# VectorE's every eighth product moved to the front of its step, with a one-element copy on GpSimd in its place there

## The chip, the cores and the metric

The kernel runs on one NeuronCore of one Trainium2 chip. The metric is device time in microseconds for one execution. Five engines matter here: TensorE (PE in the profile, with its weight loads as PEld), VectorE (DVE), ScalarE (ACT), GpSimd (POOL) and SyncE (SP), which only issues DMAs. GpSimd issues DMAs too.

## The reference

Agent attention over two batches of 12480 tokens with 49 agents, followed by a feed-forward layer whose activation is a ratio of two polynomials. Cut to what matters:

```python
a2k = softmax(scale * agents @ k.T);  agent_v = a2k @ v          # 49 x 128, per batch
x   = softmax(scale * q @ agents.T) @ agent_v                    # 24960 x 128
h   = x @ w_in                                                   # 24960 x 2048
P   = a[0] + a[1]*h + a[2]*h**2 + a[3]*h**3
Q   = 1 + abs(b[0])*abs(h) + abs(b[1])*h**2
out = (P / (Q + 1e-6)) @ w_out                                   # 24960 x 128
```

## The kernel before

**Tiles and stages.** A first stage of some 60 us computes the attention of the agents over batch 0. It also folds `agent_v` into `w_in`, so that `h` comes straight from the 49 attention weights of a token (tile `pT`) and the folded weights (`m_hi`, `m_lo`). From then on one loop does the feed-forward layer. The work is cut into 49 blocks of 512 tokens by 16 chunks of 128 hidden columns, 784 pieces, and three pieces make a **unit**: 128 partitions by 1536 elements. There are 262 units (`NU`), and step `i` of the loop starts unit `i`.

**One unit.** TensorE writes `h` into a PSUM slot (`mm1`, lines 494 and 495; there are two slots, so `mm1` of unit i+2 must wait until unit i's slot has been read). ScalarE squares it into the tile `u` (line 559). VectorE makes the denominator `w` (`dve2`, line 588) and then the first part of the numerator `u` (`dve1`, line 580); both read the slot, and `dve1` is its last reader. ScalarE turns `w` of a pair of units into its reciprocal by logarithm and exponential (lines 573 and 575). Six steps after the unit's start `u` is multiplied with `w`, and seven steps after it (`LAG`) TensorE multiplies the product with `w_out` (`mm2`, line 502).

**Who does that product.** Seven units in eight are multiplied by GpSimd (line 644, `u <- u * w`). A constant has to be added to `u` before that, and GpSimd issues an accumulating DMA for it (`add_om`, lines 600 and 605), for a pair of units at every second step; it waits for `dve1` of the younger unit of the pair. Every eighth unit (`u % 8 == 7`) and the last seven are multiplied by VectorE (`dve_last`, line 593), which adds the constant in the same instruction. Such a unit `u` is multiplied at step j = u + 6, called a **product step** here; there are 31 of them before the tail.

**Order.** The schedule is written out by hand: each engine runs its instructions in the order in which the loop names them. In a product step VectorE had: `dve2(j)`, `dve1(j)`, what `run_hold("DVE")` holds, then `dve_last(u)`. What `run_hold` runs are pieces of two side streams that `attend` spreads over the steps, one piece per step: the attention of the agents over batch 1 (scores until about 350 us, then a stage until about 600 us in which GpSimd subtracts maxima at line 253), and the attention of the tokens, in 25 groups of 1024 tokens. A group's piece on VectorE is `q_ev` (lines 422 and 423), later `q_sum` (432, 433); on GpSimd it is line 440, and a step later lines 441 and 442. A group comes every 10.67 units, so that three groups fill 32 units, and with them four product steps. The **four places** of a product step in this cycle are called D, B, A and C here, in order of time: at D, `q_ev` stands in the step's hold; at A, GpSimd has lines 441 and 442 in the step before; at C, line 440 stands in the step's hold on GpSimd.

GpSimd's queue at a product step: the product of unit u-1 (step j-1), its held pieces, nothing of its own in step j, then in step j+1 the product of unit u+1 and the `add_om` that waits for `dve1(j)`; in the queue that `add_om` stands ahead of the product.

Of the kernel before, what the change touches and what calls it, by code (L numbers as in the profile page):

```python
# [11 lines left out]
F32 = mybir.dt.float32  # L12
# [68 lines left out]
def agent_attention_rational_moe(  # L81
# [12 lines left out]
    PE, ACT, DVE, POOL, SP = nc.tensor, nc.scalar, nc.vector, nc.gpsimd, nc.sync  # L94

    const = ctx.enter_context(tc.tile_pool(name="const", bufs=1))
# [12 lines left out]
    cab = const.tile([128, 6], F32, name="cab")  # L109
    b_abs = const.tile([128, 2], F32, name="b_abs")  # L110
    cf = const.tile([128, 96], F32, name="cf")
    mcol = const.tile([128, 1], F32, name="mcol")
    flag = const.tile([128, 1], I32, name="flag")
    c0_t = const.tile([128, 1], F32, name="c0_t")
# [343 lines left out]
    NU = len(units)  # L458

    def on_pool(u):  # L460
        return u % ON_DVE != ON_DVE - 1 and u < NU - LAST_DVE

    def main(wk, streams, fast):
# [4 lines left out]
        def span(u):  # L468
            return width(units[u][0] // NFC)

        def view(k, u):
            n = len(units[u])
            if k == "w":
                return wt[u // 2 % (NWT if fast else 2)][:, u % 2, :n, :span(u)]
            if k == "x" and not fast:
                return wt[3][:, u % 2, :n, :span(u)]
            return ut[u // 2 % (NUT // 2)][:, u % 2, :n, :span(u)]
# [5 lines left out]
        def mm1(u):  # L483
            s = slots[u % 2]
            for j, n in enumerate(units[u]):
                blk, fc = divmod(n, NFC)
                f = slice(fc * 128, (fc + 1) * 128)
                t, n = blk * BT, width(blk)
                cut = min(max(N - t, 0), n)
                for b, lo, hi in ((0, 0, cut), (1, cut, n)):  # L490
                    if lo < hi:
                        assert (b, fc // 4) in made
                        rhs = pT_t[blk // 2][:, (blk % 2) * BT + lo:(blk % 2) * BT + hi]
                        PE.matmul(s[:, j, lo:hi], lhsT=m_hi[b][:KR, f], rhs=rhs, start=True, stop=False)  # L494
                        PE.matmul(s[:, j, lo:hi], lhsT=m_lo[b][:KR, f], rhs=rhs, start=False, stop=True)  # L495

        def mm2(u):
            done = None
            g = view("u", u)
            for j, n in enumerate(units[u]):  # L500
                blk, fc = divmod(n, NFC)
                PE.matmul(outs[blk % 2][:, :width(blk)], lhsT=wo[:, fc, :], rhs=g[:, j, :], start=fc == 0, stop=fc == NFC - 1)  # L502
                if fc == NFC - 1:
                    done = blk
            return done

        def out_ev(blk):
            n = width(blk)
            o = ring(at_p, 1, [128, BT], F32, "o")[:, :n]
            (DVE.tensor_copy if blk in OUT_DVE else ACT.copy)(out=o, in_=outs[blk % 2][:, :n])  # L510
            SP.dma_start(out=outT[:, blk * BT:blk * BT + n], in_=o)
# [9 lines left out]
        def run_hold(e):  # L521
            fs = hold[e]
            hold[e] = []
            for f in fs:
                f()
# [29 lines left out]
        def act(i):  # L555
            if i < NU:
                h, w, x, y = slot(i), view("w", i), view("x", i), view("u", i)
                if fast:
                    ACT.activation(out=x, in_=h, func=AF.Square, scale=arm["xb"], bias=1.0)  # L559
                else:  # L560
                    ACT.activation(out=x, in_=h, func=AF.Abs)
                    ACT.activation(out=y, in_=h, func=AF.Identity, scale=cab[:, 3:4], bias=cab[:, 2:3])
                    POOL.tensor_scalar(out=w, in0=x, scalar1=b_abs[:, 1:2], scalar2=b_abs[:, 0:1], op0=ALU.mult, op1=ALU.add)
            if fast:
                p = (i - 3) // 2
                ready = pair(p) if 0 <= p and 2 * p < NU else []
                ln, ex = i % 2 == 1, i % 2 == 0
            else:
                ready = [view("w", i - 1)] if 0 <= i - 1 < NU else []
                ln = ex = True  # L570
            for r in ready:
                if ln:
                    ACT.activation(out=r, in_=r, func=AF.Ln, bias=arm["lb"])  # L573
                if ex:
                    ACT.activation(out=r, in_=r, func=AF.Exp, scale=-1.0)  # L575

        def dve1(i):
            h, x, y = slot(i), view("x", i), view("u", i)
            if fast:
                DVE.scalar_tensor_tensor(out=y, in0=x, scalar=co["kap_l"], in1=h, op0=ALU.add, op1=ALU.mult)  # L580
            else:
                DVE.tensor_tensor(out=y, in0=h, in1=y, op=ALU.mult)
                DVE.scalar_tensor_tensor(out=y, in0=y, scalar=cab[:, 1:2], in1=h, op0=ALU.add, op1=ALU.mult)

        def dve2(i):
            h, x, w = slot(i), view("x", i), view("w", i)
            if fast:
                DVE.scalar_tensor_tensor(out=w, in0=h, scalar=co["mu_l"], in1=x, op0=ALU.max, op1=ALU.add)  # L588
            else:
                DVE.tensor_tensor(out=w, in0=w, in1=x, op=ALU.mult)  # L590

        def dve_last(u):
            DVE.scalar_tensor_tensor(out=view("u", u), in0=view("u", u), scalar=arm["om"], in1=view("w", u), op0=ALU.add, op1=ALU.mult)  # L593


        def add_om(u):
            us = [v for v in (u, u + 1) if 0 <= v < NU and on_pool(v)]
            if len(us) == 2 and all(len(units[v]) == UJ and span(v) == BT for v in us):
                t = ut[u // 2 % (NUT // 2)].rearrange("p h j t -> p h (j t)")
                POOL.dma_start(out=t, in_=omd.unsqueeze(1).to_broadcast([128, 2, UJ * BT]), accum_op=ALU.add)  # L600
                return
            for v in us:
                n, m = len(units[v]), span(v)
                src = omd.rearrange("p (j t) -> p j t", j=UJ)[:, :n, :m]
                POOL.dma_start(out=view("u", v), in_=src, accum_op=ALU.add)  # L605
# [19 lines left out]
        for i in range(NU + lag):  # L625
            act(i)
            run_hold("ACT")
            g = i - gap
            fin = [g] if 0 <= g < NU and not on_pool(g) else []
            if i == NU - 1:  # L630
                dve_last(fin.pop())
            if i < NU:
                dve2(i)
                dve1(i)
            run_hold("DVE")
            for u in fin:
                dve_last(u)
            if done is not None:
                out_ev(done)
                done = None  # L640
            if i % 2 == 0:
                add_om(i - 2)
            if 0 <= g < NU and on_pool(g):
                POOL.tensor_tensor(out=view("u", g), in0=view("u", g), in1=view("w", g), op=ALU.mult)  # L644
            run_hold("POOL")
            if i + 1 < NU:
                mm1(i + 1)
            cur = 0
            if i >= lag:
                done = mm2(i - lag)  # L650
                cur = units[i - lag][-1] // NFC
            soon = i >= lag and units[min(i + 1 - lag, NU - 1)][-1] // NFC != cur
            used = i > 0 and attend(outs[1 - cur % 2], units[min(i + 1, NU - 1)][-1] // NFC, done is not None, soon, i)
            if i < lag and not used:
                for _ in range(DUM):
                    PE.matmul(outs[0][:, :BT], lhsT=wo[:, 0, :], rhs=wi[:, :BT], start=True, stop=True)
# [85 lines left out]
    with tc.manual_schedule():  # L742
# [136 lines left out]
        def rest(fast):  # L879
            for n, d in (("q", q_t), ("pT", pT_t)):  # L880
                d.clear()
                d.update(state[n])
            for n, r in rings.items():
                r[1] = turns.get(n, 0)
            if fast:
                xb = ACT.alloc_register("xb")
                ACT.reg_load(xb, co["xb"][0:1, :].bitcast(I32))
                arm.update(om=co["om_l"], lb=co["lb_l"], xb=xb)
            else:
                arm.update(om=cab[:, 0:1], lb=c0_t)  # L890
            main(wk, [q_stream(1), w_stream(fast), a2k_stream(kv, 1, G1)], fast)
# [42 lines left out]
```

## Time and profile before

| | |
|---|---|
| median of 3 runs | 1305.13 us (1304.97 to 1305.24) |
| the profiled execution | 1304.85 us, its span 1303.1 us |
| PE busy | 1219.9 us, 94% |
| DVE busy | 1171.6 us, 90% |
| ACT busy | 1155.6 us, 89% |
| POOL busy | 1028.3 us, 79% |
| line 593, DVE, the product on VectorE | 38 instructions, 608 to 10062 ns, median 1812 ns |
| line 644, POOL, the product on GpSimd | 224 instructions, mean 3911 ns |

Four engines are busy for most of the time, and they wait for each other in a ring (slot, square, `dve2` and `dve1`, slot). So a busy share alone doesn't tell which one sets the pace; that has to be read from the stage. The median of VectorE's product is 1.81 us, its longest instance over five times that.

### The profile page before, as it was taken

The numbers are of one execution on the slowest core, as the hardware profiler recorded it, in microseconds if no ns is written. First come the engines' busy times: TensorE is split into PE (matmuls) and PEld (weight loads), VectorE is DVE, ScalarE is ACT, GpSimd is POOL, SyncE is SP. The second block draws the span as 40 slices with busy tenths as digits, with TensorE's granted clock in tenths as the row PEclk, the third lists the DMA queues.
The fourth block names the chain that finished last, engine by engine and source line by source line (L and its number), as shares of the span: only waits on it lengthen the run. The fifth ranks groups of instructions, "written<-read, shape, count | busy, mean of one in ns | idle before, by whom it ended". The sixth has DMA issues, their size and how long they took to land.

```text
span 1303.1 us, 14400 instructions
## 1 busy us (share of the span) xinstructions
PE 1219.9 (94%) x5396; PEld 711.1 (55%) x5396; DVE 1171.6 (90%) x865; ACT 1155.6 (89%) x752; POOL 1028.3 (79%) x511
## 2 busy tenths in 40 slices
PE   7979989999899989999899997999799997999998
PEld 6745545555455545555456554555455554555554
DVE  6898898998998898989999989999999989899996
ACT  3479979999799987999799997999799997999995
POOL 4538968878789887888678887888688887798893
PEclk8989989999899999999899998999899998999999
DMA  9569979998699996988879886889879886899990
GB/s 358 206 143 185 195 171 204 201 197 184 147 190 206 214 199 138 206 185 166 173 147 184 181 181 133 181 177 191 173 156 181 183 179 130 175 181 181 185 178 26
DMA packets 53263, 233.58 MB, mean 179 GB/s; under 512 B 4800, under 2 KB 5312, under 8 KB 53184
## 3 DMA queue, kind: packets, MB, share of 16 engines
q0 software_dynamic: 30720, 176.17, 70.9%
q1 hardware_dynamic: 22464, 56.39, 12.2%
q8 instruction: 45, 0.74, 0.2%
q14 instruction: 34, 0.28, 0.1%
HBM read 218.98 MB, written 13.57 MB: 178 GB/s over the span
## 4 chain that ended last, share of the span: by engine, by line
PE 71%; DVE 19%; ACT 5%; issue 2%; POOL 2%; DMA 1%; SPq 0%; DVEq 0%; ACTq 0%; POOLq 0%
PE outb L502 41%; PE slot L494 12%; PE slot L495 11%; DVE u L593 6%; DVE u L580 4%; DVE w L588 4%; ACT u L559 3%; PE outb L213 2%; POOL u L644 1%; PE outb L447 1%; ACT w L573 1%; PE outb L271 1%; DMA k<-kT 1%; PE bank L213 1%; PE outb L300 0%
## 5 line engine op out<-in xcount | busy, mean ns | idle before, releaser
L644 POOL TENSOR_TENSOR u<-u,w 128x1536 f32<-128x1536 f32 x224 | 840.4, 3911 | 0.0
L502 PE MATMUL outb<-u,wo 128*128 128x512 f32 (+1 forms) x1568 | 728.9, 601 | 49.8 <-DVE u L593 46.5
L588 DVE SCALAR_TENSOR_TENSOR w<-slot,cf,u 128x1536 f32<-128x1536 f32 (+1 forms) x262 | 472.1, 1802 | 90.2 <-ACT u L559 77.0
L502 PEld LDWEIGHTS outb<-u,wo 128*128 128x128 f32 x1568 | 299.6, 192 | 336.8 <-issue 250.2
L580 DVE SCALAR_TENSOR_TENSOR u<-u,cf,slot 128x1536 f32<-128x1536 f32 (+1 forms) x262 | 472.2, 1802 | 9.3
L559 ACT ACTIVATE u<-slot 128x1536 f32<-128x1536 f32 (+1 forms) x262 | 382.0, 1458 | 52.0 <-PE slot L495 32.8
L494 PE MATMUL slot<-pT,m_hi 113*128 113x512 f32 (+3 forms) x800 | 369.9, 464 | 14.9 <-DVE u L580 14.7
L573 ACT ACTIVATE w<-w,cf 128x3072 f32<-128x3072 f32 (+1 forms) x134 | 375.1, 2802 | 0.0
L575 ACT ACTIVATE w<-w 128x3072 f32<-128x3072 f32 (+1 forms) x134 | 362.9, 2710 | 0.0
L495 PE MATMUL slot<-pT,m_lo 113*128 113x512 f32 (+3 forms) x800 | 312.0, 391 | 0.0
L600 POOL DMA_DIRECT2D u<-omd x96 | 121.0, 1260 | 166.9 <-DVE u L580 97.6
L494 PEld LDWEIGHTS slot<-pT,m_hi 113*128 113x128 f32 x800 | 151.2, 189 | 93.5 <-DVE u L580 41.4
L495 PEld LDWEIGHTS slot<-pT,m_lo 113*128 113x128 f32 x800 | 151.5, 189 | 49.4 <-issue 25.9
L593 DVE SCALAR_TENSOR_TENSOR u<-u,cf,w 128x1536 f32<-128x1536 f32 (+2 forms) x38 | 119.2, 3147 | 0.0
L510 ACT COPY o<-outb 128x512 f32<-128x512 f32 (+1 forms) x40 | 23.6, 590 | 51.2 <-PE outb L502 51.2
L605 POOL DMA_DIRECT2D u<-omd x32 | 31.7, 990 | 40.2 <-DVE u L580 23.0
L447 PEld LDWEIGHTS outb<-ident,p 128*113 128x113 f32 x187 | 26.7, 178 | 25.2 <-issue 20.6
L213 PEld LDWEIGHTS outb<-ag,q 128*64 128x64 f32 x748 | 24.5, 141 | 17.8 <-issue 9.5
L447 PE MATMUL outb<-ident,p 128*113 128x128 f32 x187 | 28.3, 274 | 1.5 <-DVE o L510 1.5
L453 ACT CAST pT<-outb 113x512 fp32r<-113x512 f32 (+1 forms) x47 | 28.2, 600 | 0.1
L213 PE MATMUL outb<-ag,q 128*64 128x49 f32 x748 | 27.6, 228 | 0.0
L440 POOL TENSOR_TENSOR e<-e,qs 128x392 f32<-128x392 f32 (+1 forms) x25 | 26.4, 1057 | 1.5 <-DVE qs L433 0.7
(138 smaller groups left out, 476.1 us busy)
## 6 DMA issues: line engine op xcount, KB each, us to landing
u<-omd POOLq DMA_DIRECT2D x96, 1536.0 KB, 11.7
u<-omd POOLq DMA_DIRECT2D x32, 768.0 KB, 7.3
q<-qT SPq DMA_DIRECT2D x24, 512.0 KB, 7.3
outT<-o SPq DMA_DIRECT2D x48, 256.0 KB, 5.8
v<-vP SPq DMA_DIRECT2D x24, 258.0 KB, 7.1
k<-kT SPq DMA_DIRECT2D x24, 256.0 KB, 6.6
v<-vP SPq DMA_DIRECT2D x9, 645.0 KB, 11.4
k<-kT SPq DMA_DIRECT2D x8, 640.0 KB, 9.7
```

The lines of the kernel that those rows point to most:

```text
L213: PE.matmul(bank[lo:hi, o:o + A], lhsT=toks[:, lo:hi], rhs=ag[:, b * A:(b + 1) * A], start=True, stop=True)
L494: PE.matmul(s[:, j, lo:hi], lhsT=m_hi[b][:KR, f], rhs=rhs, start=True, stop=False)
L495: PE.matmul(s[:, j, lo:hi], lhsT=m_lo[b][:KR, f], rhs=rhs, start=False, stop=True)
L502: PE.matmul(outs[blk % 2][:, :width(blk)], lhsT=wo[:, fc, :], rhs=g[:, j, :], start=fc == 0, stop=fc == NFC - 1)
L559: ACT.activation(out=x, in_=h, func=AF.Square, scale=arm["xb"], bias=1.0)
L573: ACT.activation(out=r, in_=r, func=AF.Ln, bias=arm["lb"])
L575: ACT.activation(out=r, in_=r, func=AF.Exp, scale=-1.0)
L580: DVE.scalar_tensor_tensor(out=y, in0=x, scalar=co["kap_l"], in1=h, op0=ALU.add, op1=ALU.mult)
L588: DVE.scalar_tensor_tensor(out=w, in0=h, scalar=co["mu_l"], in1=x, op0=ALU.max, op1=ALU.add)
L593: DVE.scalar_tensor_tensor(out=view("u", u), in0=view("u", u), scalar=arm["om"], in1=view("w", u), op0=ALU.add, op1=ALU.mult)
L600: POOL.dma_start(out=t, in_=omd.unsqueeze(1).to_broadcast([128, 2, UJ * BT]), accum_op=ALU.add)
L644: POOL.tensor_tensor(out=view("u", g), in0=view("u", g), in1=view("w", g), op=ALU.mult)
```

## The change

`dve_last(u)` goes ahead of `dve2(j)` and `dve1(j)` in its step. Where GpSimd's own product would have been in a product step, GpSimd now copies one element of the product's result into a new tile `turn` that nobody reads; since it reads what VectorE writes, GpSimd's queue waits there until VectorE's product is done. In the last steps (i of `NU` and above) there is no copy.

```diff
+    turn = const.tile([1, 1], F32, name="turn")
...
             fin = [g] if 0 <= g < NU and not on_pool(g) else []
-            if i == NU - 1:
-                dve_last(fin.pop())
+            for u in fin:
+                dve_last(u)
             if i < NU:
                 dve2(i)
                 dve1(i)
             run_hold("DVE")
-            for u in fin:
-                dve_last(u)
             if done is not None:
                 out_ev(done)
                 done = None
+            for u in fin if i < NU else ():
+                POOL.tensor_copy(out=turn, in_=view("u", u)[0:1, 0, 0:1])
             if i % 2 == 0:
                 add_om(i - 2)
             if 0 <= g < NU and on_pool(g):
```

Line numbers below the new tile rise by one, and below the copy by one again. On VectorE, at the product step of unit 111 (a D step; numbers behind a name are buffers), the rows were before:

```order
L588 SCALAR_TENSOR_TENSOR w_756<-slot_725,cf,u_752 128x1536
L580 SCALAR_TENSOR_TENSOR u_752<-u_752,cf,slot_725 128x1536
L308 SCALAR_TENSOR_TENSOR m_lo_93<-outb_71,mcol,m_hi_91 113x512
L588 SCALAR_TENSOR_TENSOR w_756<-slot_726,cf,u_752 128x1536
L580 SCALAR_TENSOR_TENSOR u_752<-u_752,cf,slot_726 128x1536
L422 TENSOR_REDUCE qm_587<-outb_71 128x8
L423 TENSOR_TENSOR e_95<-outb_71,qm_587 128x8x49
L593 SCALAR_TENSOR_TENSOR u_749<-u_749,cf,w_757 128x1536
L588 SCALAR_TENSOR_TENSOR w_757<-slot_725,cf,u_753 128x1536
```

And there after the change:

```order
L589 SCALAR_TENSOR_TENSOR w_757<-slot_726,cf,u_753 128x1536
L581 SCALAR_TENSOR_TENSOR u_753<-u_753,cf,slot_726 128x1536
L309 SCALAR_TENSOR_TENSOR m_lo_94<-outb_71,mcol,m_hi_92 113x512
L594 SCALAR_TENSOR_TENSOR u_750<-u_750,cf,w_758 128x1536
L589 SCALAR_TENSOR_TENSOR w_757<-slot_727,cf,u_753 128x1536
L581 SCALAR_TENSOR_TENSOR u_753<-u_753,cf,slot_727 128x1536
L423 TENSOR_REDUCE qm_588<-outb_71 128x8
L424 TENSOR_TENSOR e_96<-outb_71,qm_588 128x8x49
L589 SCALAR_TENSOR_TENSOR w_758<-slot_726,cf,u_754 128x1536
```

The product has moved ahead of the step's `dve2` and `dve1` and of `q_ev`. On GpSimd, at the product step of unit 127 (an A step), the rows were before:

```order
L440 TENSOR_TENSOR e_95<-e_95,qs_871 128x8x49
L600 DMA u_749<-omd 128x2x1536
L644 TENSOR_TENSOR u_752<-u_752,w_757 128x1536
L441 TENSOR_SCALAR p_94<-e_95 128x8x49
L442 TENSOR_TENSOR p_94<-e_95,p_94 128x8x49
L600 DMA u_750<-omd 128x2x1536
L644 TENSOR_TENSOR u_753<-u_753,w_754 128x1536 x2
```

And after the change:

```order
L441 TENSOR_TENSOR e_96<-e_96,qs_872 128x8x49
L601 DMA u_750<-omd 128x2x1536
L645 TENSOR_TENSOR u_753<-u_753,w_758 128x1536
L442 TENSOR_SCALAR p_95<-e_96 128x8x49
L443 TENSOR_TENSOR p_95<-e_96,p_95 128x8x49
L641 COPY turn<-u_753 1x1
L601 DMA u_751<-omd 128x2x1536
L645 TENSOR_TENSOR u_754<-u_754,w_755 128x1536 x2
```

The copy stands behind the product of unit u-1 and what GpSimd held of the step before, and ahead of the next `add_om`. At a D step the row of GpSimd's product stands right ahead of the copy.

## Rows read from the trace of the kernel before

**Rows 1.** Who waited for whom: engine, line, releaser, us in total, times, longest

```profile
PE outb L502 <- DVE u L593: 46.5, 7, 7.7
PE slot L494 <- DVE u L580: 14.7, 15, 2.2
```

**Rows 2.** Timelines of DVE, POOL and PE at a D step: start, us, instruction, idle before

```profile
632.23 1.81 DVE L580 SCALAR_TENSOR_TENSOR u<-u,cf,slot 128x1536 f32<-128x1536 f32 x1
634.55 0.57 DVE L423 TENSOR_TENSOR e<-outb,qm 128x392 f32<-128x392 f32 x1
635.03 9.25 DVE L593 SCALAR_TENSOR_TENSOR u<-u,cf,w 128x1536 f32<-128x1536 f32 x1
644.21 1.80 DVE L588 SCALAR_TENSOR_TENSOR w<-slot,cf,u 128x1536 f32<-128x1536 f32 x1
646.05 1.81 DVE L580 SCALAR_TENSOR_TENSOR u<-u,cf,slot 128x1536 f32<-128x1536 f32 x1
...
634.57 1.21 POOL L600 DMA_DIRECT2D u<-omd  x1 [4.41 <-DVE qm L422]
635.34 7.32 POOL L644 TENSOR_TENSOR u<-u,w 128x1536 f32<-128x1536 f32 x2
...
644.34 5.17 PE L502 MATMUL outb<-u,wo 128*128 128x512 f32 x6 [5.95 <-DVE u L593]
```

**Rows 3.** Timelines of DVE and POOL at a B step

```profile
818.14 1.81 DVE L580 SCALAR_TENSOR_TENSOR u<-u,cf,slot 128x1536 f32<-128x1536 f32 x1
823.88 1.81 DVE L593 SCALAR_TENSOR_TENSOR u<-u,cf,w 128x1536 f32<-128x1536 f32 x1
...
816.71 4.01 POOL L644 TENSOR_TENSOR u<-u,w 128x1536 f32<-128x1536 f32 x1
...
824.49 1.21 POOL L600 DMA_DIRECT2D u<-omd  x1 [3.77 <-DVE u L580]
```

**Rows 4.** Timeline of DVE, its products alone, in two stretches

```profile
168.34 9.27 DVE L593 SCALAR_TENSOR_TENSOR u<-u,cf,w 128x1536 f32<-128x1536 f32 x1
212.49 1.81 DVE L593 SCALAR_TENSOR_TENSOR u<-u,cf,w 128x1536 f32<-128x1536 f32 x1
...
324.72 9.27 DVE L593 SCALAR_TENSOR_TENSOR u<-u,cf,w 128x1536 f32<-128x1536 f32 x1
...
782.50 9.23 DVE L593 SCALAR_TENSOR_TENSOR u<-u,cf,w 128x1536 f32<-128x1536 f32 x1
...
928.28 9.60 DVE L593 SCALAR_TENSOR_TENSOR u<-u,cf,w 128x1536 f32<-128x1536 f32 x1
```

**Rows 5.** Windows: us, busy us of PE, PEld, DVE, ACT, POOL; clock, DMA

```profile
212.00:250.00 38.00, 38.00 (x215) 22.07 (x214) 35.02 (x30) 36.00 (x26) 31.15 (x14) 1.00 0.93 205
858.00:893.00 35.00, 34.34 (x137) 19.84 (x137) 32.39 (x22) 34.84 (x22) 29.73 (x12) 1.00 0.89 183
```

**Rows 6.** Windows, POOL's busy us, from a product step's DMA to next u-1

```profile
928.20:967.22 39.02, 31.06 (x14) 0.87 0.69 140
970.98:1002.40 31.42, 29.62 (x13) 1.00 0.89 182
1005.57:1036.63 31.06, 28.97 (x12) 1.00 0.87 178
893.80:924.05 30.25, 30.16 (x13) 1.00 0.88 178
...
368.27:400.50 32.23, 31.23 (x16) 1.00 0.93 202
478.53:519.41 40.88, 33.21 (x19) 0.92 0.76 163
1221.95:1252.45 30.50, 30.39 (x14) 1.00 0.87 165
```

**Rows 7.** Timeline of POOL ahead of an A step

```profile
1002.98 0.96 POOL L442 TENSOR_TENSOR p<-e,p 128x392 fp32r<-128x392 f32 x1
```

**Rows 8.** POOL's groups of instructions, shapes apart: count, busy us, mean ns

```profile
L318 POOL TENSOR_SCALAR cf<-cf 128x1 f32<-128x1 f32 x22 | 5.6, 265 | 3.8 <-DVE cf L318 2.9
```

## The prediction

> **What bounds the kernel now.** I began with who waits for whom. TensorE stood idle for 46.5 us in front of `mm2` for VectorE's product, in only seven waits of up to 7.7 us [rows 1]. So a few of the 31 products are very late, and the timeline of one shows why [rows 2]. `dve1` ended at 634.04. GpSimd's `add_om`, which had waited for it, started 0.53 us later, at 634.57. VectorE was still at `q_ev` then, and its product was issued only at 635.03. GpSimd ran two products back to back, until 642.66, and VectorE's product, 1.81 us long elsewhere, ended at 644.28: 1.62 us after GpSimd had stopped. TensorE idled 5.95 us for it. At a B step nothing stands between `dve1` and the product; it starts at 823.88, 0.61 us ahead of the DMA, and takes 1.81 us [rows 3]. So the two products, each with both inputs in SBUF, exclude each other; whoever comes first keeps the other out, and GpSimd keeps it across back-to-back instructions. `q_ev` makes VectorE second at all seven D steps.
>
> Away from these steps the pace is set elsewhere: from 212 to 250 us TensorE is busy for 38.00 of 38 us, and from 858 to 893 us ScalarE for 34.84 of 35 [rows 5]. VectorE's idle time there is worth nothing by itself.
>
> What a D step costs is read from the starts of the products, eight units apart. From 168.34 to 212.49 are 44.15 us, from there to 324.72 three intervals of 37.41 on average: 6.74 too long [rows 4]. From 782.50 to 823.88 are 41.38 us, and to 928.28 three of 34.80: 6.58 too long [rows 3, 4]. The wait, the lower clock after it (0.87 over that stretch against 1.00 in the others [rows 6]) and what was caught up again are all in it. Three D steps lie in the first half and four in the second.
>
> **The change, part by part.**
>
> *The seven waits go.* At the front of its step the product has neither `q_ev` nor a waiting `add_om` before it, and the copy keeps GpSimd from starting anything new until it is done. Removed: 3 x 6.74 + 4 x 6.58 = 46.5 us.
>
> *What it meets at the front.* At the B step `dve1(j-1)` ended at 819.95, but GpSimd was in the product of u-1 until 820.72 [rows 3]. VectorE would wait for that and end at 820.72 + 1.62 = 822.34. Then come `dve2` and `dve1`, 3.65 us together (644.21 to 647.86 [rows 2]): the slot is free at about 825.9, where it was free before the product's start at 823.88. So all 31 product steps hand TensorE its slot about 2 us later, and `mm1(j+2)` and then the square behind it come late. `mm2(u)`, behind that `mm1` in TensorE's queue, has its product long before. A wait of seven steps is replaced by a short one of all.
>
> *A ring that closes.* This is the cost that I take as the main one. Before, `dve1(j)` did not depend on GpSimd. Now it stands behind the product, the product behind GpSimd's work up to the product of u-1, and that work behind the `add_om` that waited for the `dve1` of the last product step. An interval between two product steps can't be shorter than 0.53 (from `dve1` to the DMA) + W (what GpSimd has to do until u-1 is done) + 1.62 - 0.07 (`dve2` starts at 644.21, the product ended at 644.28) + 3.65 = W + 5.73 us [rows 2]. W is GpSimd's busy time in these stretches, idle time left out [rows 6]:
> - D to B: 31.06, ring 36.8
> - B to A: 29.62, ring 35.35. Lines 441 and 442 stand ahead of the copy there; they end at 1003.94 [rows 7], 1.54 us after the stretch's end at 1002.40. If VectorE can't get in before them, 36.9. I take the middle, 36.1, since no row shows a product that waits behind that pair.
> - A to C: 28.97, ring 34.7
> - C to D: 30.16, ring 35.9
>
> Against 34.80, which ScalarE allows, that is +2.0, +1.3, 0 and +1.1: 4.4 us for four intervals, 17.6 us for the four rounds of the second half. The last stretch gives 30.39, ring 36.1, +1.3. In the first half TensorE's 37.41 covers the rings of these four kinds. Only between about 325 and 600 us, with line 253 on GpSimd too, W is 31.23 to 33.21, ring 37.0 to 38.9, and a tail at A; I take 1 us for each of the five intervals in which that shows, 5 us (bounds 0 and 10). Together 23.9 us given back.
>
> *The copy.* The nearest row is a GpSimd instruction of one element per partition, 265 ns [rows 8]. It lies in time in which GpSimd waits anyway: the next `add_om` needs `dve1(j)`, 3.65 + 0.53 us after the product. So nothing is added; uncovered it would be 31 x 0.27 = 8 us. Behind it in GpSimd's queue are that `add_om`, and at some steps line 440 or 253, which fit into the same gap and whose readers come a step or more later. The copy would be missed only there: the `add_om` is already held back by the new place of `dve1(j)`.
>
> *The rest.* The tail's products and SyncE's queue stay as they were.
>
> The sum: the profiled execution took 1304.85 us, 0.3 below the median of the runs. 1304.85 - 46.5 + 23.9 = 1282 us.
>
> A rule of the Trainium skill bears on the B-to-A term. "SBUF — State Buffer", section "Who interferes with whom", says that VectorE instructions with two SBUF inputs and GpSimd instructions that read SBUF take a shared pair of ports in turn, for a whole instruction, and that the one that issues second waits until the first is done. By that letter VectorE would get in after one GpSimd instruction. The trace agrees on who excludes whom, but not on when it ends: the product of [rows 2] waited through a pair of GpSimd products. By the rule B to A is 35.35 and the sum some 4 x 0.75 = 3 us lower, 1279; by the row up to 3 us higher, 1285. I stay between.
>
> **The rivals.**
> - *The full gain.* The ring doesn't bind, because VectorE gets its turn between GpSimd's instructions or GpSimd's work packs closer once its waits for `dve1` go. For it: TensorE's intervals in the first half leave room. Against it: GpSimd is busy for 29 to 31 us of a second-half interval of 34.8, and the product with `dve2` and `dve1` needs more than 5 of them [rows 6]. Time: 1304.85 - 46.5 = 1258, to 1266 with some of the short waits. Chance 0.17.
> - *The ring eats the gain (slower or no change).* Place: GpSimd's work between the copy and u-1. The 31 intervals have to grow by 46.5 / 31 = 1.5 us on average, where I have 23.9 / 31 = 0.8. If the held pieces or the handing over of the port add 1.54 us (the pair of lines 441 and 442) to each of the 17 intervals of the second half, where nothing covers it, the time is 1282 + 26 = 1308. For it: all the rings lie within 2.1 us of the pace now, with no slack left. Against it: three of the four W are measured without such a pair at their end. Chance 0.14 for slower, 0.06 for within 0.2% (2.6 us), which is about what a measurement of this kernel can tell from no change.
> - *The clock falls at the new waits.* TensorE's longest wait for `dve1` was 2.2 us [rows 1]; at A steps it could now be 3 or more. After the seven long waits the clock was 0.87 over 39 us, 5 us of TensorE's full-clock time [rows 6]. Four A steps in the second half: up to 20 us, 1302. For it: the waits come in every interval. Against it: they are half as long as those seven. Chance 0.06.
> - *The change does less than it says.* Without the copy the product at the front would keep most of its gain; that changes the reason, not the time.
>
> **How the numbers follow.** The ring that binds in part: 0.57, its own range 1270 to 1294 (half and one and a half times the 23.9). With the others the range that leaves out 2 in 10 runs from 1260 into the case of the clock, 1302. Faster by over 0.2%: 0.57 + 0.17 + 0.06 = 0.80; within 0.2%: 0.06; slower: 0.14.
>
> **What would show it.** Right: no product on VectorE much over 4 us and none of the seven waits; the granted clock at 1.00 through the loop; VectorE's products 2 to 4 us long, ending 1.6 us after GpSimd's product of u-1; GpSimd without idle time but in the gap of about 5.8 us at the copy; intervals near 37.4 in the first half and 35.9 in the second. Wrong: products that wait through two GpSimd products again; long GpSimd work ahead of the copy; intervals of 34.8 in the second half (then the ring doesn't bind) or of 36.5 and more (then it eats the gain); a lower clock behind each product step.

## The result, and the profile after

| | before | after |
|---|---|---|
| median | 1305.18 us (1304.97 to 1306.49, 4 runs) | 1285.67 us (1283.42 to 1287.32, 4 runs) |
| profiled execution, its span | 1304.85 us, 1303.1 us | 1287.32 us, 1285.5 us |
| mean granted clock | 0.972 | 0.986 |

The ratio is 0.9848, with a 95% interval of 0.9833 to 0.9862: 19.5 us less. The forecast was 1282.

The seven long waits of [rows 1] are gone: the view of waits has no line any more in which TensorE itself waits for VectorE's product. What grew is the short wait for the slot (lines with their us, times, longest; a line numbered 494 before is line 495 here, as every line below the new tile is one further down): first after the change, of TensorE and of its weight loads, then the weight loads before.

```profile
PE slot L495 <- DVE u L581: 35.8, 28, 2.9
PEld slot L495 <- DVE u L581: 68.1, 67, 3.7
```

```profile
PEld slot L494 <- DVE u L580: 41.4, 51, 3.0
```

TensorE's own wait was 14.7 us in 15 waits [rows 1], so each is a little longer and there are nearly twice as many. The groups of instructions, with shapes kept together, give the product on VectorE, the copy, and GpSimd's product:

```profile
L645 POOL TENSOR_TENSOR u<-u,w 128x1536 f32<-128x1536 f32 x224 | 856.5, 4034 | 0.0
L594 DVE SCALAR_TENSOR_TENSOR u<-u,cf,w 128x1536 f32<-128x1536 f32 (+2 forms) x38 | 100.0, 2643 | 0.0
L641 POOL COPY turn<-u 1x1 f32<-1x1 f32 x32 | 6.1, 192 | 39.2 <-DVE u L594 39.2
```

The copy itself costs 192 ns, and GpSimd stood 39.2 us before it. A B step of the second half, which answers to [rows 3], shows the ring. Timelines of DVE, POOL, PE and ACT (start, us, instruction, idle before):

```profile
788.64 1.82 DVE L581 SCALAR_TENSOR_TENSOR u<-u,cf,slot 128x1536 f32<-128x1536 f32 x1
790.37 5.05 DVE L594 SCALAR_TENSOR_TENSOR u<-u,cf,w 128x1536 f32<-128x1536 f32 x1
795.34 1.81 DVE L589 SCALAR_TENSOR_TENSOR w<-slot,cf,u 128x1536 f32<-128x1536 f32 x1
797.18 1.81 DVE L581 SCALAR_TENSOR_TENSOR u<-u,cf,slot 128x1536 f32<-128x1536 f32 x1
...
789.39 4.40 POOL L645 TENSOR_TENSOR u<-u,w 128x1536 f32<-128x1536 f32 x1
795.48 0.18 POOL L641 COPY turn<-u 1x1 f32<-1x1 f32 x1 [1.69 <-DVE u L594]
799.53 1.21 POOL L601 DMA_DIRECT2D u<-omd  x1 [3.87 <-DVE u L581]
...
799.05 0.50 PE L495 MATMUL slot<-pT,m_hi 113*128 113x512 f32 x1 [1.93 <-DVE u L581]
799.39 0.40 PE L496 MATMUL slot<-pT,m_lo 113*128 113x512 f32 x1
...
800.34 0.63 PE L495 MATMUL slot<-pT,m_hi 113*128 113x512 f32 x1
...
801.50 1.45 ACT L560 ACTIVATE u<-slot 128x1536 f32<-128x1536 f32 x1 [2.28 <-PE slot L496]
```

VectorE's product was issued at 790.37, GpSimd's product of u-1 ended at 793.79, VectorE's at 795.42: 1.63 us later. The slot became free at 798.99, TensorE had waited 1.93 us for it, and ScalarE then 2.28 us for TensorE. The matmul at 799.39 took 0.40 us, the one at 800.34 took 0.63: the granted clock had fallen to half, 1.2 GHz (window as in [rows 5]):

```profile
799.80:803.20 3.40, 3.40 (x7) 1.99 (x7) 2.95 (x3) 1.70 (x2) 3.40 (x2) 0.50 0.52 70
```

The records show this four times in the loop, behind the B steps at 799, 946 and 1093 us and behind one A step at 837.

Where the time came from is read from the ends of `dve1(j)` in the product steps (start plus duration of line 581 in the timeline, line 580 before). The table gives, in us, the four values of each kind of interval in the second half (units 111 to 239). The last column is the kernel of the third experiment below, in which `dve1` waits for no work of GpSimd:

| | before | after | product ahead of the held piece |
|---|---|---|---|
| D to B | 43.61, 42.46, 43.15, 43.13 | 36.94, 36.86, 37.22, 36.85 | 36.51, 34.06, 34.06, 34.43 |
| B to A | 34.90, 34.58, 34.60, 35.53 | 36.14, 37.34, 37.26, 38.70 | 34.92, 34.59, 34.59, 35.52 |
| A to C | 34.71, 34.74, 34.72, 34.92 | 35.48, 36.75, 35.28, 35.11 | 34.72, 34.73, 34.73, 34.92 |
| C to D | 34.24, 34.01, 34.01, 34.07 | 36.05, 36.07, 36.07, 36.41 | 34.26, 34.02, 34.02, 34.10 |
| all 16 | 587.38 | 584.53 | 554.18 |
| first half, units 15 to 111 | 466.70 | 448.11 | 444.82 |

So the gain is 18.6 us in the first half and 2.9 us in the second, where the D-to-B intervals win 24.5 us and the other three kinds give 21.6 us of it back. Ahead of unit 15 and behind unit 239 are lost 3.9 us. Together 17.6, the difference of the spans.

### The profile page after: what moved, and what is told of

The parts are those of the page before. It is cut to its first block, busy times and chain, and to the rows that moved or that the text cites. A ratio compares the mean times of both kernels' runs of the same rounds, so it can differ in the third digit from the quotient of the medians.

```text
span 1285.5 us, 14429 instructions
## 1 busy us (share of the span) xinstructions
PE 1218.1 (95%) x5396; PEld 707.7 (55%) x5396; DVE 1151.0 (90%) x865; ACT 1158.2 (90%) x752; POOL 1046.1 (81%) x543
## 4 chain that ended last, share of the span: by engine, by line
PE 51%; DVE 24%; POOL 11%; issue 7%; ACT 6%; DMA 1%; SPq 0%; DVEq 0%; ACTq 0%; POOLq 0%
PE outb L503 28%; PE slot L495 9%; DVE w L589 9%; DVE u L581 9%; POOL u L645 8%; PE slot L496 8%; ACT u L560 4%; PE outb L214 2%; DVE u L594 1%; ACT w L574 1%; PE outb L448 1%; POOL u L601 1%; PE outb L272 1%; ACT pT L454 1%; PE outb L301 1%
## 5 line engine op out<-in xcount | busy, mean ns | idle before, releaser
L645 POOL TENSOR_TENSOR u<-u,w 128x1536 f32<-128x1536 f32 x224 | 856.5, 4034 | 0.0
L503 PE MATMUL outb<-u,wo 128*128 128x512 f32 (+1 forms) x1568 | 718.5, 594 | 8.4 <-POOL u L645 5.0
L503 PEld LDWEIGHTS outb<-u,wo 128*128 128x128 f32 x1568 | 295.6, 190 | 292.7 <-issue 244.4
L495 PE MATMUL slot<-pT,m_hi 113*128 113x512 f32 (+3 forms) x800 | 370.7, 465 | 35.9 <-DVE u L581 35.8
L601 POOL DMA_DIRECT2D u<-omd x96 | 126.7, 1320 | 136.0 <-DVE u L581 77.3
L594 DVE SCALAR_TENSOR_TENSOR u<-u,cf,w 128x1536 f32<-128x1536 f32 (+2 forms) x38 | 100.0, 2643 | 0.0
L606 POOL DMA_DIRECT2D u<-omd x32 | 39.4, 1232 | 0.0
L641 POOL COPY turn<-u 1x1 f32<-1x1 f32 x32 | 6.1, 192 | 39.2 <-DVE u L594 39.2
L442 POOL TENSOR_SCALAR p<-e 128x392 fp32r<-128x392 f32 (+1 forms) x25 | 37.3, 1493 | 0.1
L214 PEld LDWEIGHTS outb<-ag,q 128*64 128x64 f32 x748 | 24.5, 141 | 17.8 <-issue 7.9
L441 POOL TENSOR_TENSOR e<-e,qs 128x392 f32<-128x392 f32 (+1 forms) x25 | 30.0, 1199 | 0.1
```

## The experiments

The first four separate the two parts of the change and try a third place; the last four test the ring. The diffs are shortened and are against the changed kernel. The kernel before took 1305.34 us in the session of the first four and 1305.21 us in that of the others.

**The copy alone**, with the product where it was before:

```diff
-            for u in fin:
-                dve_last(u)
+            if i == NU - 1:
+                dve_last(fin[0])
             if i < NU:
                 dve2(i)
                 dve1(i)
             run_hold("DVE")
+            for u in fin if i != NU - 1 else ():
+                dve_last(u)
```

> VectorE's product back at its old place behind the step's hold, the copy on GpSimd kept. My theory: the seven long waits come from GpSimd's constant-adding DMA and products getting in while VectorE is at the token stream's maxima; the copy alone forbids that. And since dve1 is no longer behind the product, the ring through GpSimd stays open. So the gain of 46.5 us comes whole but for GpSimd starting 1.3 to 2.9 us later at each product step: 1258 to 1270 us, no product on VectorE over 2 us. Rival (the new place is what helps, the copy is idle): the seven waits stay, 1300 to 1308 us.

Measured: 1260.47 us (1260.10 to 1260.81), ratio 0.9657 [0.9641, 0.9673]. The copy alone brings 44.9 us, more than twice the whole change. GpSimd now waits at the copy for VectorE's product also where the held piece delays that, and at none of the 31 product steps ahead of the tail is the product shut out: it took 1.81 us at each. (The one in the loop's last step, which stands at the front in every kernel here, took 3.63.)

**The place alone**, without the copy (its two lines taken out):

> The product at the front of its step as in the change, without the copy on GpSimd. My theory: the next constant-adding DMA waits for dve1, which stands behind the product, so the copy is idle but at the steps where line 440 or 253 is next in GpSimd's queue; 1283 to 1290 us, within 0.4% of the changed kernel. Rival (GpSimd must be stopped by the copy): at C steps the product waits behind line 440 too and the gain shrinks by 1 to 2 us a step there and where line 253 follows, 1295 to 1305 us.

Measured: 1287.43 us (1286.50 to 1289.04), ratio 0.9864 [0.9848, 0.9881]. That can't be told from the whole change. The copy does nothing that counts when the product stands at the front, and the front costs what it costs with the copy or without.

**A third place**: behind `dve1`, but ahead of the held piece, and no copy:

```diff
-            for u in fin:
-                dve_last(u)
+            if i == NU - 1:
+                dve_last(fin[0])
             if i < NU:
                 dve2(i)
                 dve1(i)
+            for u in fin if i != NU - 1 else ():
+                dve_last(u)
             run_hold("DVE")
...
-            for u in fin if i < NU else ():
-                POOL.tensor_copy(out=turn, in_=view("u", u)[0:1, 0, 0:1])
```

> The order dve2, dve1, product, hold, and no copy: only the token stream's pieces are moved behind the product. My theory: the product is then always 0.5 us ahead of the constant-adding DMA that waits for dve1, at D steps as at the others, so all seven waits go and no ring closes: 1258 to 1264 us. Rival (GpSimd's work or TensorE and ScalarE together set the pace anyway, so the whole 46.5 us can't be had): 1275 to 1290 us.

Measured: 1249.49 us (1249.01 to 1250.70), ratio 0.9573 [0.9557, 0.9589], the fastest of all kernels here and 8.5 us below the range that I had expected, since the seven waits had cost more than I had read. At the D step of [rows 2] DVE and POOL now read:

```profile
610.50 1.81 DVE L581 SCALAR_TENSOR_TENSOR u<-u,cf,slot 128x1536 f32<-128x1536 f32 x1
612.24 1.81 DVE L594 SCALAR_TENSOR_TENSOR u<-u,cf,w 128x1536 f32<-128x1536 f32 x1
613.97 0.56 DVE L423 TENSOR_REDUCE qm<-outb 128x8 f32<-128x392 f32 x1
...
612.85 1.21 POOL L601 DMA_DIRECT2D u<-omd  x1 [4.40 <-DVE u L581]
613.62 7.38 POOL L645 TENSOR_TENSOR u<-u,w 128x1536 f32<-128x1536 f32 x2
```

The product is there 0.61 us ahead of the DMA, as at the B step of [rows 3], and GpSimd's pair starts when VectorE is nearly done.

The rows of the kernel before say more exactly what "first" means. In [rows 2] VectorE's product was issued 0.31 us ahead of GpSimd's pair by the records (635.03 and 635.34) and came second all the same; what was ahead of it was `add_om` (634.57). So it is at all seven late products: 0.09 to 0.47 us behind the start of `add_om`, 0.31 to 0.69 us ahead of the start of the pair. At the other 24 product steps ahead of the tail VectorE's product was issued before `add_om` and took 1.81 us. One of these is a D step, the last, with a short `q_ev`; there 0.04 us were enough (DVE and POOL of the kernel before):

```profile
1221.91 1.81 DVE L593 SCALAR_TENSOR_TENSOR u<-u,cf,w 128x1536 f32<-128x1536 f32 x1
...
1221.95 1.21 POOL L600 DMA_DIRECT2D u<-omd  x1 [3.40 <-DVE qm L422]
```

Whether the DMA issue itself keeps VectorE out, or the pair behind it, these rows don't show.

In the new order nothing closes a ring: `dve1` waits for no GpSimd work, and the pace is ScalarE's and TensorE's again (windows: us, busy us of PE, PEld, DVE, ACT, POOL; clock):

```profile
752.72:786.78 34.06, 32.94 (x103) 18.68 (x102) 32.10 (x22) 33.81 (x21) 31.06 (x14) 1.00 0.87 180
786.78:821.37 34.59, 34.53 (x135) 19.41 (x134) 32.33 (x23) 34.32 (x20) 31.12 (x14) 1.00 0.93 192
```

This is also the measure of what the seven waits had cost: against the kernel before it wins 55.85 us, and the seven D-to-B intervals shrink by 7.30, 7.63, 7.83, 7.10, 8.40, 9.09 and 8.70, together 56.05.

**The third place with the copy:**

> The same order as in the run before it, dve2, dve1, product, hold, with the copy on GpSimd. My theory: the copy holds the constant-adding DMA back by 1.3 us at each product step, which GpSimd's slack at that place takes up; 1258 to 1268 us, 0 to 4 us above the run without it. Rival (the copy protects something that the order alone doesn't): clearly faster than the run without it, by over 3 us.

Measured: 1259.34 us (1257.07 to 1260.02), ratio 0.9643 [0.9626, 0.9660]: here the copy costs 9.9 us, where I had expected 4 at most. In the waits, this kernel's `mm2` for GpSimd's products first, then the same line without the copy:

```profile
PEld outb L503 <- POOL u L647: 17.5, 30, 1.5
```

```profile
PEld outb L503 <- POOL u L645: 1.9, 5, 0.8
```

GpSimd starts its next `add_om` only when VectorE's product is done and copied: in one step `dve1` ended at 755.94 and `add_om` began at 757.98, 2.04 us later, where 0.53 had been enough. Every product behind it comes that much later, and TensorE's weight loads wait for one of them 30 times. So a copy that holds GpSimd is free only where its start was late already.

**More work for GpSimd.** Five memsets of a small tile that nothing else touches, once in each product interval, in the changed kernel:

```diff
+            if fast and g >= 0 and g % ON_DVE == 2 and i < NU:
+                for _ in range(5):
+                    POOL.memset(pad, 0.0)
             if 0 <= g < NU and on_pool(g):
```

> The changed kernel, with five memsets of a 128x113 tile on GpSimd added once in every product interval (ahead of GpSimd's product of the units u with u mod 8 = 2), about 5 x 0.19 = 0.94 us of GpSimd time in each of some 30 intervals. They touch nothing that the product or the other engines use. Theory (the closed ring sets the interval, because VectorE's product waits for GpSimd's product before it and GpSimd's copy for VectorE's): the added time goes into the interval wherever GpSimd was idle only at the copy, that is the D-to-B and C-to-D intervals and those of the stage with line 254, some 12 to 20 intervals, so +10 to +19 us: 1295 to 1305. Rival (the ring is no bound, VectorE's product simply holds its own stream back by a fixed amount at each step): the same additions cost what they cost in the kernel with the product behind the multiply, 0 to +3 us: 1285 to 1289.

Measured: 1309.19 us (1306.95 to 1311.71), ratio 1.0028 [1.0018, 1.0038] to the kernel before: 23.5 us more than the changed kernel, 4 us above the range that I had expected, and the gain is gone. The memsets were longer than I had estimated:

```profile
L647 POOL MEMSET pad<- 128x113 f32 x160 | 51.6, 323 | 7.4
```

That is 1.6 us in an interval, of which the stretches below show about 1.1. Not all of the 23.5 us is the ring: in the profiled execution the clock fell seven times in the loop, where it fell four times in the changed kernel; at the 1.6 us a fall worked out in the next section that is an estimated 5 us. **The control** is the same edit in the kernel of the third place:

> The control of the run before: the same five memsets in the same place, in the kernel with the product between line 581's multiply and VectorE's held work and no copy (1249.5 us in the earlier session). Theory of the ring: nothing there closes a ring, GpSimd has idle time in each interval and takes the 0.94 us out of it: 0 to +4 us, 1249 to 1254. Rival (GpSimd's load as such is what costs): as much here as in the changed kernel, +10 us or more: 1259 or above.

Measured: 1253.71 us (1252.33 to 1254.72), ratio 0.9609 [0.9593, 0.9625]: 4.2 us more. The same edit costs 5.6 times as much where the ring is closed, and still some four times without those 5 us. That rules out GpSimd's load as such.

**Less work for GpSimd.** The changed kernel without the pieces of lines 441 to 443 for the groups after the first:

```diff
-            yield (None, None, [("POOL", lambda bk: q_split(g)[0]())])
-            yield (None, None, [("POOL", lambda bk, j=j: q_split(g)[j]()) for j in (1, 2)])
+            yield (None, None, [])
+            yield (None, None, [])
```

> The changed kernel without the three GpSimd pieces (lines 441 to 443) that normalise and split the token attention weights of each group after the first: that part of the computation is left out, about 4.6 us of GpSimd's work in one interval of four (A to C). Theory of the ring: the A step's product no longer meets line 442, and one interval in four loses GpSimd work; the A-to-C interval was already not bound by the ring (GpSimd idle 0.5 to 2.1 us in it), so little comes of it: -2 to -8 us, 1278 to 1284, while D-to-B and C-to-D stay at 36 to 37 us. Rival (the pieces and the product's waits through them at A are what costs): the difference to the kernel with the product behind the multiply falls from 36 to under 20 us: 1268 or less.

Measured: 1279.43 us (1276.40 to 1279.74), ratio 0.9804 [0.9788, 0.9820], 6.2 us less. The number lies in what I had expected, but not for my reason, in two ways. The pieces do not lie between A and C alone: by the changed kernel's timeline three lie between D and B, two behind the DMA between C and D, and the others late in the intervals B to A and A to C. The two kinds that I had expected to stay at 36 to 37 fell, C to D to 34.60 to 34.92 and D to B to 34.67 to 35.23 (without the first). And the whole second half took 567.87 us, 16.7 less than in the changed kernel, 12.0 of it in these two kinds and most of the rest in B to A, where the clock no longer fell; a single stall ahead of unit 111 took most of that away again. It stands in the last section. **Its control:**

> The control of the run before: the kernel with the product between line 581's multiply and VectorE's held work and no copy, without the same three GpSimd pieces of the groups after the first (the same part of the computation left out). Both theories: GpSimd has idle time there, 0 to -4 us from 1249.5 us: 1245 to 1250.

Measured: 1259.77 us (1251.94 to 1262.14), ratio 0.9656 [0.9640, 0.9672], 10 us above the range that I had expected; the runs scatter. The profiled one is the fastest of them (1251.94), and its second half is 554.11 us, as without the edit (554.18). Where the others lose time no trace shows. So the loss of the second half against the third place falls from 30.4 us (584.53 - 554.18) to 13.8 (567.87 - 554.11) when GpSimd has less to do. By the medians the difference to the control is 19.7 us, just under the 20 that I had named as the rival's mark, so this pair of times does not decide between the ring and the rival. The intervals do: B to A, where the rival's pieces stand ahead of the product, took 35.70 without them and, in the front without the copy, 35.65 with them (both at a clock of 1.00, windows in the next section).

**The ring, measured in three kernels.** From the DMA behind a product step to the end of GpSimd's product u-1 (windows of POOL: us, busy, clock), D to B and C to D: of the changed kernel,

```profile
762.66:793.79 31.13, 31.04 (x14) 1.00 0.81 162
873.62:903.95 30.33, 30.25 (x13) 1.00 0.81 157
```

of the one with more work,

```profile
774.25:806.55 32.30, 31.99 (x19) 1.00 0.79 155
886.39:917.81 31.42, 31.10 (x18) 1.00 0.83 154
```

and of the one with less:

```profile
768.26:797.20 28.94, 28.80 (x11) 1.00 0.88 175
873.91:902.77 28.86, 28.77 (x11) 1.00 0.86 172
```

With the prediction's 5.73 us added to the first column they give 36.86 and 36.06, 38.03 and 37.15, 34.67 and 34.59. The intervals measured were 36.86 and 36.07, 38.04 and 37.16, 34.67 and 34.60. The sum alone is no proof: it comes out wherever VectorE's product waits for u-1 and the DMA starts 0.53 us after `dve1`, in B to A too. What shows that the ring is the pace is that GpSimd is idle for 0.08 to 0.31 us at most in these stretches, and that they move with GpSimd's work.

## Why the prediction was right, and where only its sizes cancelled

**"The seven waits go": right, sized too small.** 46.5 us were forecast, 56 measured in the third place. Two choices made it small. The step measured from the start of the product that was itself late (782.50, while `dve1` ended at 781.50), which gave 41.38 us for an interval of 42.46. And it took off the mean of the other three kinds, 34.80; this interval without its wait is the shortest together with C to D, 34.06.

**"What it meets at the front": right in the mechanism, not priced.** The product waits for GpSimd's product of u-1 and ends 1.62 to 1.65 us after it at the D, B and A steps of the second half, but for the first D step, where it was not held. But the step handed TensorE its slot two microseconds late in every product step and charged nothing for it beyond the ring. That is the part of the loss that failed: from B to A GpSimd was idle for 0.35 to 3.3 us before its product of u-1 was done, so the ring did not bind there, and still the intervals are 1.2 to 3.2 us longer than in the third place. ScalarE, busy for 34.32 of 34.59 us there in the third place, stood still for TensorE's late start (2.28 us in the timeline above) and can make up little of it, as I read it. Windows from `dve1` to `dve1`, B to A: first the changed kernel, then the same interval in two kernels in which the clock stayed up, the one with less GpSimd work and the front without the copy.

```profile
798.99:836.33 37.34, 35.85 (x132) 20.18 (x132) 33.42 (x23) 33.20 (x19) 32.73 (x15) 0.95 0.85 175
```

```profile
802.40:838.10 35.70, 34.00 (x132) 19.39 (x132) 33.31 (x23) 34.46 (x20) 29.08 (x12) 1.00 0.91 182
```

```profile
800.99:836.64 35.65, 34.16 (x132) 19.29 (x132) 33.33 (x23) 33.12 (x19) 32.62 (x14) 1.00 0.92 185
```

With the clock at 1.00 the interval is 35.65 to 35.70, with 0.95 it is 37.34. So of the 2.75 us that it lost against 34.59 about 1.1 are the wait and 1.6 the clock.

**"A ring that closes": right, and 0.05 to 0.5 us short where it binds** (D to B: 36.8 forecast, 36.85 to 37.22 measured; C to D below). The longest of them are those in which the DMA started 0.91 us after `dve1` and not 0.53. Its price was too small, because it too was counted from 34.80. C to D: 35.9 forecast, 36.05 to 36.41 measured, but from a base of 34.02 to 34.26, so 8.2 us for four and not 4.4. D to B: 8.8 for 8.0. B to A: 9.8 for 5.2, by the other cause. A to C: 3.5 for 0, 2.0 of it in the one interval with the clock at 0.95. Together 30.4 us in the second half for 17.6; in the first half 3.3 for 5, ahead of it and behind it 3.9 for 1.3. So what is given back is 37.6 us between the two spans, not 23.9.

**The sum** came out within 4 us because two terms were small by about the same amount: 46.5 - 23.9 = 22.6 forecast, 55.9 - 36.2 = 19.7 by the medians. The base of 34.80 is in both; a mean over three intervals stood where each kind has its own. In D to B it is in the gain and in what is given back, and drops out; in the other kinds it does not. The halves show that the rest was luck: forecast were gains of 15.2 us in the first and 8.7 in the second and a loss of 1.3 outside them, measured 18.6, 2.9 and 3.9. By the prediction's own marks the second half, at 36.5 us an interval (584.53 / 16), showed that the ring eats the gain there. The first half decided the sign.

**The copy: right.** At the front it costs nothing and brings nothing that can be measured. The prediction's reason, that the new place of `dve1` already holds `add_om` back, is what the second run shows. At the two places behind `dve1` the copy costs about 10 us or brings 45, each by holding GpSimd.

**The rule of the Trainium skill.** "SBUF — State Buffer", section "Who interferes with whom", lets the second engine in after one instruction. At the A steps it was so. DVE and POOL there:

```profile
829.86 2.89 DVE L594 SCALAR_TENSOR_TENSOR u<-u,cf,w 128x1536 f32<-128x1536 f32 x1
...
827.18 3.94 POOL L645 TENSOR_TENSOR u<-u,w 128x1536 f32<-128x1536 f32 x1
830.63 2.48 POOL L442 TENSOR_SCALAR p<-e 128x392 fp32r<-128x392 f32 x1
833.20 0.96 POOL L443 TENSOR_TENSOR p<-e,p 128x392 fp32r<-128x392 f32 x1
```

GpSimd's product ended at 831.12 and VectorE's at 832.75, while line 442 stood from 830.63 to 833.11 and let VectorE through: 2.48 us, where its mean in the kernel of the third place is 0.96. So the tail term at A was nothing, and the ring there 35.35, as by the rule; the middle that I took, 36.1, had no ground. But [rows 2] and the stall of the last section show products that did not let VectorE in, so the rule is not the whole of it.

**The rivals.** The full gain did not come, since the ring binds in half of the second half's intervals. The clock did fall behind four new waits, three at B steps and one at an A step, where that rival had all four, and cost about 1.6 us each, some 6 us, not 20. Each fall came within 1 us behind a wait of TensorE for the slot, of 1.48 to 2.96 us. But the wait alone does not decide it. The front without the copy waited as long at the same step, and its clock stayed up:

```profile
801.05 0.50 PE L495 MATMUL slot<-pT,m_hi 113*128 113x512 f32 x1 [1.92 <-DVE u L581]
```

In the changed kernel a wait of 2.36 us at 1238 brought no fall either. What decides stays open; a run that fills the wait was not tried. The products were up to 5.40 us long, not 4.

## What to carry to other kernels

When two engines exclude each other, put the shared instruction where it wins by being issued first (here one place earlier in its own queue and so ahead of the other engine's DMA issue, 55.9 us), before making either engine wait for the other. A wait added on an engine that the pace-setting chain now runs through closes a ring: its length is that engine's whole work between two waits plus the fixed handovers, and each microsecond put into it costs. Price every kind of interval against its own undisturbed length, not against the mean of the kinds.

## What the runs showed that was not expected

A small VectorE instruction can be shut out for longer than any product of [rows 4]. In the changed kernel with less GpSimd work, a 49x128 TENSOR_SCALAR of the attention over batch 1 met GpSimd's products. DVE, POOL and PE:

```profile
578.30 12.22 DVE L291 TENSOR_SCALAR av_acc<-av_acc,avr,cf 49x128 f32<-49x128 f32 x1
...
575.43 7.32 POOL L645 TENSOR_TENSOR u<-u,w 128x1536 f32<-128x1536 f32 x2
582.23 1.39 POOL L606 DMA_DIRECT2D u<-omd  x1
582.85 7.59 POOL L645 TENSOR_TENSOR u<-u,w 128x1536 f32<-128x1536 f32 x2
...
590.58 0.34 PE L294 MATMUL outb<-ident,av_acc 49*128 49x49 f32 x1 [11.23 <-DVE av_acc L291]
```

It waited through the rest of one pair, through a DMA issue and a second pair, and ended 0.08 us after GpSimd's last product (590.44); TensorE lost 11.2 us. In the changed kernel the same instruction took 1.18 us, in the profiled run of the control 2.82 us: there it ended at 582.86, 0.10 us after GpSimd's pair (582.76), and the next product began only at 583.17, 0.41 us after the pair; in the stalled case it began 0.10 us after. In these two cases a pause of GpSimd let VectorE in and a bare handover from one product to the next did not. What decides at the A steps, where line 442 had begun by its record and yet came second, stays open.
